# Pooled attention and sticky expert routing: another order of issue in the attention, and a new expert's first weights split ahead of the turning of the next rows

## The chip, the cores and the metric

The kernel runs on one core of one Trainium2 chip. The metric is the device time of one execution in microseconds (us); the number given for a kernel is the median of its runs. The core has five engines with an instruction stream each: PE (TensorE), DVE (VectorE), ACT (ScalarE), POOL (GpSimd) and SP (SyncE, which here only starts DMA transfers). Streams wait for one another by semaphores.

## The reference, cut to what matters

Attention runs over keys and values that are averaged in groups of 8 along the sequence; its output x (8 x 576 rows of 512) goes through a mixture of 8 experts. A token takes the expert of its own argmax, or that of the token before it, by a local gate. All is fp32.

```python
# q, k, v: 8 batches x 8 heads x 576 x 64; k_p, v_p: means over groups of 8 (72 left)
scores = scale * q @ k_p.T;  attn = softmax(scores);  x = attn @ v_p
logits = x @ w_gate;  local = sigmoid(x @ w_local)
for b in range(8):
    prev_e = -1
    for s in range(576):
        fresh_e = argmax(logits[b, s])
        e = fresh_e if s == 0 or local[b, s] < 0.5 else prev_e
        prev_e = e
        h = maximum(x[b, s] @ w1[e], 0)        # w1[e]: 512 x 1024
        out[b, s] = softmax(logits[b, s])[e] * (h @ w2[e])   # w2[e]: 1024 x 512
```

## The kernel before

**Three stages.** The attention takes the span's first 245 us or so. Blocks of 256 tokens of the most populous expert follow, in code written out (to about 315 us), and then a loop of 20 blocks over all experts.

**The attention's order of issue** is a list of words, `PLAN`, which `run(PLAN)` walks: `do(op, n)` issues one small step, and every engine executes its own instructions in the order in which the list puts them. There are 20 units, five for each pair of batches. A word is a step and a number: `lq`, `lk`, `lv` load a unit's data (SP's queue); `vp`, `vt`, `vc`, `vm`, `vl`, `vd` make pooled values and their routing logits (`vaug`); `kp` pools keys; `sc`, `mx`, `sb`, `ex` are scores, maximum, subtraction and exponential (ACT L508); `T0` to `T2` turn the probabilities on PE, `T0c` and so on copy the turned ones (`aT`, ACT L376); `v0` to `v2` multiply by the values (PE L566), `v0c` and so on copy the results (`osb`); `fs`, `fp`, `fd` sum, scale and store rows of x. A `.d` or `.p` behind the name puts a step on DVE or POOL instead of its usual engine.

Routing words stand among them, per pair of batches: `rA` (argmax and gate as small DVE operations, L621 to L636, with transposes on PE L645) to `rP` (places of tokens), then `s`, the scatters of row ids (POOL L702). `ch` and `er` choose the most populous expert; `w1`, `w2` load its weights and `p1`, `p2` split them: ACT rounds them to a high part (L212, L217), and POOL subtracts to get the low part (L213, L218). `il`, `ga` load the ids of a static block and gather its rows (POOL L270), `XR` reorders the gathered rows on ACT (L281), `X0`, `X1` turn and split them for PE. `XR:0` is the first static block, `XR:1` the second. `PLAN_B` and `PLAN_C` list the static blocks in the same way.

Every fp32 product is made from three products of high and low parts, so an expert block needs x and the weights split.

**The loop.** A block is two groups of 128 rows, or one. Its steps, in the order of the code: `l1_two` or `l1_one` (first layer, PE L330 and L332, or L957 and L963), `next_x` for the block to come (DVE turns its gathered rows, L318; ACT and DVE split them, L323 and L324; DVE sums the ids of the block after that, L304 and L305), `fetch` (eight gathers of that later block on POOL, L314), and `rest` (second layer in two halves, PE L351; scaling, DVE L1065; scattered stores on POOL, L1076). Where the next block has another expert, `rest` also splits the new weights behind the second half of the second layer, `weights1` (ACT L212 and DVE L213) and then `weights2` (ACT L217 and DVE L218), inside an `If`, and starts the loads of the expert after that. Every engine in the `If` reads the flag `chg` from a table and branches on it, whether the expert changes or not.

Of the kernel before, what the change touches and what calls it, by code (L numbers as in the profile page):

```python
# [51 lines left out]


PLAN = plan("""
wa:0 lv:0 lv:1 wa:1 lv:2 lk:0 lk:1 lq:0 lk:2 lq:1 lq:2 lc:0 lq:3 pf:0 vp:2 vt:2 vc:2 vm:2 kp:0 vp:0 lk:3 kp:1 vp:1
lv:3 vt:0 lk:4 sc:0 vc:0 vm.d:0 mx:0 lv:4 vt:1 lv:5 lq:4 vm:1 sb:0 kp:2 ex:0 sc:2 lk:5 vl:0 T0:0 vd:0 mx:2 vl:2
T0c:0 vc:1 vd:2 T1:0 sb:2 vl:1 T1c:0 T2:0 vd:1 T2c:0 ex:2 v0:0 kp:3 v1:0 v0c:0 lk:6 vp.d:3 v1c:0 v2:0 lv:6 vt:3
v2c:0 sc:1 vm:3 vc:3 fs:0 vl:3 fp:0 mx:1 lq:5 lq:6 T0:2 vp:5 T0c:2 T1:2 vd:3 sb:1 vt:5 T1c:2 v0:2 vm:5 vc:5 fd:0
vp:4 vl:5 v0c:2 T2:2 vd:5 v1:2 kp:4 ex:1 lv:7 vt:4 lv:8 lk:7 vp:6 vc:4 vm.d:4 T2c:2 vl:4 v1c:2 T0:1 vd:4 kp:5 T0c:1
T1:1 lv:9 kp:6 lk:8 T1c:1 T2:1 v2:2 T2c:1 sc:3 v2c:2 lk:9 fs:2 v0:1 lq:7 mx:3 fp:2 v0c:1 v1:1 fd.p:2 sb:3 vp:8 v1c:1  # L60
v2:1 sc:4 v2c:1 ex:3 fs:1 vt:6 lq:8 vt:8 mx:4 fp:1 vc:6 vc:8 T0:3 sb:4 vm:8 fd:1 vm:6 T0c:3 T1:3 kp:7 vp:7 T1c:3
T2:3 vl:6 T2c:3 sc:5 vd:6 ex:4 lk:10 T0:4 mx:5 vp:9 lv:10 lv:11 lq:9 T0c:4 T1:4 vl:8 T1c:4 vt:7 vd:8 sb:5 vc:7 v0:3
vm:7 lv:12 kp:8 v0c:3 v1:3 ex:5 lk:11 v2:3 v1c:3 vl:7 v2c:3 v0:4 fs:3 v0c:4 v1:4 vd:7 fp:3 T0:5 v1c:4 fs:4 fd.p:3
T0c:5 T1:5 rA:0 fp:4 T1c:5 T2:5 sc:6 fd.p:4 T2c:5 vp:11 vt:9 lq:10 mx:6 vt:11 vc:9 vl:9 vc:11 vm:11 rT0:0 vm:9 vd:9
sb:6 vl:11 vp:10 rT1:0 vd:11 ex:6 rS0:0 v0:5 rS1:0 vp:12 lv:13 lv:14 kp:9 v0c:5 v1:5 v1c:5 v2:5 lv:15 lk:12 vt:10
v2c:5 T0:6 vm:10 vc:10 fs:5 vl:10 T0c:6 T1:6 vd:10 fp:5 v0:6 T1c:6 vp:14 fd:5 kp:10 T2:6 v0c:6 v1:6 vp:13 T2c:6
lk:13 v1c:6 v2:6 rT2:0 v2c:6 lv:16 sc:7 lv:17 fs:6 rS2:0 fp:6 lq:11 mx:7 rE:0 rL:0 fd.p:6 sb:7 vt:12 vt:13 vm:12
rO:0 ex:7 sc:8 vm:13 vp:17 rR:0 vc:12 mx:8 lq:12 vc:13 T0:7 vp:15 rV:0 T0c:7 T1:7 v0:7 T1c:7 rP:0 lv:18 T2:7 v0c:7
v1:7 sb:8 s:0 T2c:7 v1c:7 v2:7 s:0 kp:11 ex:8 sc:9 s:0 mx:9 lq:13 lk:14 v2c:7 T0:8 s:0 fs:7 T0c:8 T1:8 s:0 sb:9 v0:8
T1c:8 fp:7 T2:8 s:0 v0c:8 fd:7 v1:8 T2c:8 ex:9 s:0 v2:8 v1c:8 s:0 T0:9 v2c:8 fs:8 s:0 T0c:9 T1:9 vl:12 sc:10 T1c:9  # L70
vd:12 fp:8 v0:9 fd.p:8 mx:10 lq:14 v0c:9 v1:9 sb:10 vl:13 v1c:9 vt:14 vt:15 vc:14 vm:14 fs:9 sc:11 ex:10 vd:13 fp:9
rA:1 fd.p:9 vl:14 vc:15 T0:10 vm:15 lq:15 vp:16 T0c:10 T1:10 vd:14 mx:11 v0:10 T1c:10 T2:10 sb:11 v0c:10 vp:18 v1:10
lv:19 lv:20 T2c:10 v1c:10 v2:10 ex:11 vl:15 lv:21 vt:16 vd:15 vt:17 vm.d:16 sc:12 vm:17 v2c:10 vc:16 fs:10 vc:17
vl:16 lq:16 T0:11 vd:16 fp:10 mx:12 vl:17 T0c:11 T1:11 fd.p:10 vd:17 sb:12 v0:11 vp:20 T1c:11 T2:11 kp:12 vp:19
v0c:11 v1:11 T2c:11 ex:12 kp:13 lk:15 v2:11 rT0:1 v1c:11 lv:22 lv:23 v2c:11 fs:11 rT1:1 sc:13 rS0:1 fp:11 rS1:1
fd.p:11 rT2:1 lq:17 T0:12 rS2:1 mx:13 rE:1 vp:23 T0c:12 T1:12 rL:1 T1c:12 sb:13 vp:21 T2:12 v0:12 T2c:12 rO:1 ex:13
rR:1 v1:12 rV:1 v0c:12 v1c:12 v2:12 rP:1 T0:13 v2c:12 s:0 ch:0 T0c:13 T1:13 s:0 v0:13 fs:12 T1c:13 er:0 s:0 T2:13
kp:14 v0c:13 v1:13 fp:12 T2c:13 w1:0 w2:0 w1:1 v1c:13 v2:13 s:0 fd:12 sc:14 v2c:13 s:0 fs:13 vt:18 lq:18 vt:19
vc:18 s:0 vl:18 mx:14 vt:20 p1:0 w1:2 sb:14 vc:19 vd:18 sc:15 p2:0 vm.d:20 vm.d:18 vm.d:19 ex:14 vl:19 mx:15 p1:1 w1:3
lq:19 T0:14 vd:19 T0c:14 sb:15 p1:2 vc:20 kp:15 T1:14 T1c:14 v0:14 ex:15 v1:14 v0c:14 vl:20 v1c:14 T0:15 vd:20 fs:14  # L80
s:0 p1:3 T1:15 rA:2 T0c:15 sc:16 T1c:15 T2:15 vt:21 T2c:15 mx:16 s:0 vt:23 vc:21 vl:21 vc:23 rT0:2 s:0 vd:21 sb:16
vl:23 fp:13 rT1:2 il:0 il:1 vd:23 ex:16 vm.d:23 fp:14 sc:17 fd:13 vm:21 fd:14 rS0:2 T0:16 rS1:2 ga:0 XR:0 T0c:16
T1:16 mx:17 T1c:16 T2:16 T2c:16 sb:17 v0:15 vp:22 v0c:15 v1:15 ex:17 v2:15 w2:1 w2:2 w2:3 v1c:15 vt:22 v2c:15 rT2:2
vm:22 vc:22 fs:15 vl:22 T0:17 vd:22 fp:15 rS2:2 v0:16 p2:1 fd:15 v1:16 v0c:16 p2:2 v2:16 v1c:16 T1:17 p2:3 sc:18
v2c:16 rE:2 fs:16 T0c:17 T1c:17 rL:2 mx:18 T2:17 v0:17 T2c:17 rO:2 fp:16 sb:18 v0c:17 v1:17 fd.p:16 rR:2 v1c:17
v2:17 ex:18 rV:2 X1:0 X1c:0 T0:18 v2c:17 sc:19 T0c:18 fs:17 X0:0 X0c:0 T1:18 fp:17 v0:18 T1c:18 fd.p:17 rP:2 T2:18
v0c:18 v1:18 mx:19 s:0 T2c:18 sb:19 v1c:18 v2:18 s:0 ex:19 s:0 v2c:18 T0:19 fs:18 s:0 T0c:19 T1:19 T1c:19 v0:19 s:0
v0c:19 v1:19 s:0 v1c:19 s:0 ga:1 XR:1 ma:0 fs:19 s:0 s:0 fp:18 fp:19 fd:18 fd:19
""")
# [12 lines left out]
def moe_attention(ctx: ExitStack, tc: tile.TileContext, q, q_st, k, v, w_gate, w_local, w1, w2, out):  # L102
# [1017 lines left out]
    def weights1(nx):  # L1120
        for c in range(KD):
            split1(rw1(c), c, nc.vector)
        load1(rw1, nx)
# [3 lines left out]
            split2(rw2(c), c, nc.vector)  # L1127
        load2(rl2, nx)

    def rest(j, single):  # L1130
# [15 lines left out]
        with tc.If(chg > 0):  # L1146
# [73 lines left out]
```

## Time and profile before

| what | value |
|---|---|
| median of 3 runs (lowest, highest) | 791.36 us (790.5, 796.12) |
| profiled execution: its time, its span | 789.34 us, 786.9 us |
| mean granted TensorE clock | 0.899 |
| stages of the span | attention to 245, static blocks to 315, loop to 787 us |
| blocks in the loop | 20, of which 5 with one group of rows |
| changes of expert among them | 6, before the blocks that start at 412, 479, 525, 551, 643 and 661 us |

A row of the timeline gives the start, the duration, the engine, the line in the kernel, the operation with its tiles and shapes, the count, and in brackets the idle time of the engine ahead of it with what ended it. A row of the windows view gives a stretch, its length, the busy time and count of PE, PEld (weight load), DVE, ACT and POOL, the granted clock, the share of DMA time and GB/s. "PEclk" on the page is the granted clock of each fortieth of the span in tenths. Times are from the start of the span.

### The profile page before, as it was taken

Reading aid. Unit: us, or ns where it says so; the run is one execution under the profiler, and the core shown is the slowest. Engines: PE = TensorE matmul, PEld = TensorE weight load, DVE = VectorE, ACT = ScalarE, POOL = GpSimd, SP = SyncE. Lnnn points to the kernel's source line nnn. Section 1 sums busy time; section 2 is a strip of 40 time slices with the busy share of each in tenths; the row PEclk is TensorE's granted clock in tenths of the full one; section 3 lists DMA queues with packets and bytes.
Section 4 is the critical chain, followed back from the end, with each engine's and each line's share of the span. In section 5 each row is a group of like instructions: output and inputs, shape, how many; then the busy total and the mean of one; then the engine's idle time right before and its main releaser. Section 6 shows DMA issues by size and latency. Waiting matters only on the chain. (4 is left out here: it accounts for less than half of the span.)

```text
span 786.9 us, 14972 instructions
## 1 busy us (share of the span) xinstructions
PE 657.8 (84%) x3588; PEld 545.8 (69%) x3589; DVE 450.9 (57%) x1058; ACT 273.8 (35%) x613; POOL 437.8 (56%) x659
## 2 busy tenths in 40 slices
...
PEclk9998779866798999899999899899989997999995
...
GB/s 236 284 317 248 234 174 180 146 202 54 122 54 67 31 203 106 44 41 42 42 56 242 52 36 213 83 91 197 256 54 35 42 132 223 176 50 42 42 41 29
DMA packets 49377, 96.77 MB, mean 123 GB/s; under 512 B 22974, under 2 KB 22978, under 8 KB 49348
## 3 DMA queue, kind: packets, MB, share of 16 engines
...
q8 instruction: 14, 0.23, 0.1%
...
## 5 line engine op out<-in xcount | busy, mean ns | idle before, releaser
L314 POOL DMA_INDIRECT kt<-x_rows,idk x168 | 180.1, 1072 | 49.7 <-issue 43.4
L330 PE MATMUL hp<-x,w1h 128*128 128x512 f32 x376 | 147.1, 426 | 11.7 <-ACT w1h L212 5.0
L351 PE MATMUL o_ps<-w2h,ht_h 128*128 128x512 f32 x312 | 123.9, 397 | 2.7 <-PEq L1140 1.0
L351 PE MATMUL o_ps<-w2l,ht_h 128*128 128x512 f32 x312 | 122.8, 394 | 0.0
L351 PE MATMUL o_ps<-w2h,ht_l 128*128 128x512 f32 x312 | 122.8, 394 | 0.0
L332 PE MATMUL hp<-x,w1l 128*128 128x256 f32 x376 | 112.4, 299 | 8.0 <-DVE w1l L213 3.1
L330 PEld LDWEIGHTS hp<-x,w1h 128*128 128x128 f32 x376 | 76.5, 204 | 32.5 <-issue 11.2
L338 DVE TENSOR_TENSOR hs<-hp,hs 128x256 f32<-128x256 f32 x94 | 39.2, 423 | 100.1 <-ACT hs L337 66.3
L337 ACT COPY hs<-hp 128x256 f32<-128x256 f32 x94 | 34.3, 367 | 165.3 <-PE hp L332 46.1
L332 PEld LDWEIGHTS hp<-x,w1l 128*128 128x128 f32 x376 | 76.8, 204 | 13.4 <-issue 12.7
L566 PE MATMUL op<-vaug,aT 128*128 128x148 f32 (+4 forms) x448 | 75.4, 346 | 4.1 <-ACT aT L376 4.0
L566 PEld LDWEIGHTS op<-vaug,aT 128*128 128x128 f32 (+1 forms) x448 | 69.3, 208 | 9.5 <-ACT aT L376 5.2
L351 PEld LDWEIGHTS o_ps<-w2h,ht_h 128*128 128x128 f32 x312 | 59.5, 191 | 16.9 <-issue 4.5
L342 ACT ACTIVATE ht_h<-hs 128x256 fp32r<-128x256 f32 x136 | 57.0, 419 | 35.4 <-DVE hs L338 21.3
L351 PEld LDWEIGHTS o_ps<-w2h,ht_l 128*128 128x128 f32 x312 | 59.3, 190 | 12.8 <-DVE ht_l L343 0.2
L351 PEld LDWEIGHTS o_ps<-w2l,ht_h 128*128 128x128 f32 x312 | 59.5, 191 | 11.7
L1065 DVE TENSOR_SCALAR ob<-o_ps,m_a 128x512 f32<-128x512 f32 x42 | 31.4, 749 | 59.1 <-PE hp L332 16.2
L343 DVE SCALAR_TENSOR_TENSOR ht_l<-hs,ht_h 128x256 fp32r<-128x256 f32 x136 | 57.0, 419 | 8.0 <-ACT ht_h L342 7.1
L1086 POOL TENSOR_TENSOR kt<-idk,zf 128x8 f32<-128x8 f32 x20 | 8.6, 432 | 90.4 <-DVE idk L305 86.5
L1076 POOL DMA_INDIRECT out<-ob,m_e x42 | 44.8, 1067 | 25.0 <-issue 25.0
L702 POOL DMA_INDIRECT ids<-pm,pos x36 | 35.5, 988 | 19.1 <-DVE pos L699 9.4
L323 ACT CAST x<-qt 128x512 fp32r<-128x512 f32 x40 | 22.8, 618 | 60.3 <-DVE qt L318 60.3
...
## 6 DMA issues: line engine op xcount, KB each, us to landing
...
```

What stands on the lines that cost most here:

```text
L314: nc.gpsimd.indirect_dma_start(out=xk[:, j, :], out_offset=None, in_=x_pc[0:4 * rows], in_offset=bass.IndirectOffsetOnAxis(ap=idk[:, j:j + ...
L330: nc.tensor.matmul(out=ps, lhsT=W1[0][:, kk, f * P:(f + 1) * P], rhs=xt[:, kk].rearrange("p i n -> p (i n)"), start=(kk == 0), stop=False, ...
L332: nc.tensor.matmul(out=ps[:, 0:2 * P], lhsT=W1[1][:, kk, f * P:(f + 1) * P], rhs=xt[:, kk, 0, :], start=False, stop=(kk == KD - 1), skip_g ...
L337: nc.scalar.copy(out=hb[:, 0, :], in_=ps[:, 2 * P:])
L338: nc.vector.tensor_tensor(out=hb[:, 1, :], in0=ps[:, 0:2 * P], in1=hb[:, 0, :], op=ALU.add)
L342: nc.scalar.activation(out=ht[0][:, f, :], in_=hb, func=AF.Relu)
L343: nc.vector.scalar_tensor_tensor(out=ht[1][:, f, :], in0=hb, scalar=0.0, in1=ht[0][:, f, :].bitcast(F32), op0=ALU.max, op1=ALU.subtract)
L351: nc.tensor.matmul(out=to[h], lhsT=ht[i][:, kk, h * P:(h + 1) * P], rhs=W2[j][:, kk, :], start=(n == 0), stop=(n == 3 * KF - 1))
L566: nc.tensor.matmul(out=out, lhsT=lhs, rhs=rhs if len(out.shape) == 3 else rhs.rearrange("p s x -> p (s x)"), start=all(x[0] != n for x in ...
L702: nc.gpsimd.indirect_dma_start(out=ids[u % 4].rearrange("t m w -> (t m) w"), out_offset=bass.IndirectOffsetOnAxis(ap=pos[:, u:u + 1], axis=0),
L1065: nc.vector.tensor_scalar(out=ob[:, h, :], in0=o_ps[h], scalar1=m_a[:, h, 1:2], scalar2=None, op0=ALU.mult)
L1076: nc.gpsimd.indirect_dma_start(out=outv, out_offset=bass.IndirectOffsetOnAxis(ap=m_e[h][:, 0:1], axis=0), in_=ob[:, h, :], in_offset=None, ...
```

## The change

**The list.** `PLAN` is written in another order, with the same steps, and `XR:1` moves from its end to `PLAN_B`, behind `rO:3`. Some steps go to another engine: on balance one `vp` and three `vm` more stand on DVE, and one `fd` more on POOL. The new text is one line longer, so every later line number is one higher, and nine higher at the end. One line of it, where the first static block's rows are gathered and reordered:

```diff
@@ PLAN (all of its lines differ; one is shown)
+v1:14 T1c:15 T2:15 w1:3 vl:21 v1c:14 sc:17 vd:21 T2c:15 ex:16 fs:14 vl:23 ga:0 fp:14 vd:23 p1:2 v0:15 rA:2 T0:16
+v0c:15 p1:3 v1:15 T0c:16 T1:16 v1c:15 mx:17 XR:0 v2:15 rT0:2 fd:14 v2c:15 sb:17 T1c:16 rT1:2 vp:22 rS0:2 fs:15
...
@@ PLAN_B
-L1:4 rR:3 ct:0 rV:3 rP:3 h0:4 h1:4 s:0 s:0 s:0 s:0 s:0 s:0 s:0 s:0 s:0 L1:5 tc:0 cn:0 i1:0 h0:5 h1:5
+XR:1 L1:4 rR:3 ct:0 rV:3 rP:3 h0:4 h1:4 s:0 s:0 s:0 s:0 s:0 s:0 s:0 s:0 s:0 L1:5 tc:0 cn:0 i1:0 h0:5 h1:5
```

**The loop.** The flag is read right behind the first layer, and `weights1` is done there, ahead of `next_x`; `weights2` stays where it was.

```diff
-    def rest(j, single):
-        chg = entry(j + 1, 2, (EN.Activation, EN.DVE, EN.Pool, EN.SP), 1)
-        nx = entry(j + 1, 3, (EN.SP,), E - 1)
+    def changes(j):
+        return entry(j + 1, 2, (EN.Activation, EN.DVE, EN.SP), 1), entry(j + 1, 3, (EN.SP,), E - 1)
+
+    def first(chg, nx):
+        with tc.If(chg > 0):
+            weights1(nx)
+
+    def rest(j, single, chg, nx):
         meta_shift()
...
         with tc.If(chg > 0):
-            weights1(nx)
             weights2(nx)
...
     l1_two()
+    chg, nx = changes(1)
+    first(chg, nx)
     next_x()
     fetch(1)
-    rest(1, None)
+    rest(1, None, chg, nx)
...
+            chg, nx = changes(iv)
+            first(chg, nx)
             next_x()
             fetch(iv)
-            rest(iv, two)
+            rest(iv, two, chg, nx)
```

**ACT's instructions around `XR:0`.** `at` are probabilities, `aT` the turned ones, `osb` results of the attention, `brow` a row of the routing. Before:

```order
L508 ACTIVATE at<-ap 128x2x2x216
L508 ACTIVATE at<-ap 128x2x80
L508 ACTIVATE at<-ap 128x128
L648 COPY brow<-tp 2x256
L281 COPY qt<-qt 128x4x4x32 x2
L376 COPY aT<-tp 128x512 x2
L376 COPY aT<-tp 128x128
L376 COPY osb<-op 128x444
```

ACT in the changed kernel, at the same copies of the gathered rows (now L282):

```order
L213 CAST w1h<-kt 128x1024
L377 COPY osb<-op 128x444
L213 CAST w1h<-kt 128x1024
L377 COPY aT<-tp 128x512
L377 COPY osb<-op 128x444
L282 COPY qt<-qt 128x4x4x32 x2
L377 COPY osb<-op 128x2x148
L377 COPY aT<-tp 128x512
```

Five copies of ACT, of which two are splits of weights, now stand between the point of the gather and the copies of the gathered rows; before, none did.

**POOL's instructions around the splits of the first expert's weights.** `ids` are the scattered row ids, `w1l` and `w2l` the low parts, `xs` scaled rows of x, `vaug` the pooled values; the last row is the gather of the first static block. Before:

```order
L702 DMA ids_65<-pm,pos 65536x2
L213 TENSOR_TENSOR w1l<-kt,w1h 128x1024
L218 TENSOR_TENSOR w2l<-vt_in,w2h 128x1024
L213 TENSOR_TENSOR w1l<-kt,w1h 128x1024 x2
L702 DMA ids_66<-pm,pos 65536x2
L213 TENSOR_TENSOR w1l<-kt,w1h 128x1024
L702 DMA ids_67<-pm,pos 65536x2
L702 DMA ids_64<-pm,pos 65536x2
L603 TENSOR_TENSOR xs<-osb,rr 128x512
```

POOL in the changed kernel, from the last scatter of the second pair on:

```order
L703 DMA ids_64<-pm,pos 65536x2
L214 TENSOR_TENSOR w1l<-kt,w1h 128x1024
L445 TENSOR_TENSOR vaug_210<-vs,mk 128x2x64
L604 TENSOR_TENSOR xs<-osb,rr 128x512
L214 TENSOR_TENSOR w1l<-kt,w1h 128x1024
L219 TENSOR_TENSOR w2l<-vt_in,w2h 128x1024
L267 MEMSET qt 128x1024
L271 DMA qt<-x_rows,idr_191 128x512 x2
L604 TENSOR_TENSOR xs<-osb,rr 128x256
L214 TENSOR_TENSOR w1l<-kt,w1h 128x1024 x2
```

Four splits stood in a row among the scatters; now all scatters of that pair come first, three splits come ahead of the gather and two right behind it, beside the routing of the third pair.

**DVE's instructions in the loop**, from the end of a first layer on. Before, the turning of the next rows (L318) is the first thing after the branch of the first layer, and the splits (L213) come behind the scaling (L1065):

```order
L1177 UNCONDITIONAL_BRANCH
L318 REGISTER_ALU
L318 STREAM_TRANSPOSE qt<-kt 128x8x4x32
...
L1065 TENSOR_SCALAR ob<-o_ps_2481,m_a 128x512
L1146 COMPARE_AND_BRANCH
L213 REGISTER_ALU
L213 TENSOR_TENSOR w1l<-raw_3004,w1h 128x1024
```

DVE in the changed kernel:

```order
L1184 UNCONDITIONAL_BRANCH
L224 ISA
L224 TENSOR_LOAD tab
L1135 COMPARE_AND_BRANCH
L214 REGISTER_ALU
L214 TENSOR_TENSOR w1l<-raw_3001,w1h 128x1024
...
L1135 UNCONDITIONAL_BRANCH
L319 REGISTER_ALU
L319 STREAM_TRANSPOSE qt<-kt 128x8x4x32
```

A read of the flag and a branch now stand ahead of the turning in every block, and four subtractions more where the expert changes; the branch behind the scaling is still there, for `weights2` alone.

More of the change, by code (lines that the diff above doesn't have):

```diff
@@ L85 @@
[L85 to L88, printed above, removed]
+wa:0 lv:0 lv:1 lv:2 lk:0 wa:1 lk:1 lk:2 lq:0 lc:0 lq:1 lq:2 pf:0 lq:3 vp:0 vp.d:2 lv:3 vt:0 vc:0 vm:0 vt:2 kp:0
@@ new lines @@
+vc:2 vm:2 vp:1 lk:3 kp:1 lv:4 vt:1 lv:5 kp:2 vm:1 lk:4 sc:0 lk:5 vl:0 mx:0 lq:4 vc:1 vd:0 sb:0 vl:2 vd:2 ex:0 vl:1
+sc:2 vd:1 T0:0 mx:2 T0c:0 T1:0 vp:3 sb:2 v0:0 T1c:0 T2:0 kp:3 v1:0 v0c:0 T2c:0 lv:6 vt:3 v1c:0 v2:0 vm.d:3 vp:5
+vc:3 lk:6 vl:3 v2c:0 sc:1 vp:4 ex:2 vd:3 fs:0 vt:5 lq:5 lq:6 T0:2 mx:1 vc:5 fp:0 lv:7 lv:8 vt:4 vl:5 vm.d:5 vc:4
+vm:4 T0c:2 vd:5 kp:4 vl:4 fd.p:0 T1:2 vd:4 vp:6 v0:2 kp:5 lk:7 T1c:2 T2:2 v0c:2 v1:2 T2c:2 kp:6 lv:9 lk:8 v1c:2
+v2:2 sb:1 lk:9 vt:6 v2c:2 vm:6 fs:2 ex:1 sc:3 fp:2 vc:6 mx:3 lq:7 T0:1 vp:8 T1:1 T0c:1 sb:3 fd.p:2 v0:1 T1c:1 vp:7
@@ new lines @@
+T2:1 kp:7 v1:1 v0c:1 T2c:1 ex:3 v2:1 vp:9 lv:10 lv:11 lk:10 v1c:1 sc:4 v2c:1 T0:3 lq:8 fs:1 vl:6 lv:12 T0c:3 T1:3
+vd:6 vt:8 fp:1 mx:4 T1c:3 vm.d:8 vc:8 sb:4 T2:3 fd.p:1 vt:7 T2c:3 kp:8 vl:8 vc:7 sc:5 vm:7 ex:4 vd:8 kp:9 lk:11
+v0:3 lq:10 T0:4 v0c:3 mx:5 vp:11 lk:12 v1:3 T0c:4 vp:10 T1:4 sb:5 v1c:3 v2:3 T1c:4 vl:7 v2c:3 vt:9 vd:7 ex:5 vt:11
+fs:3 sc:6 lv:14 lv:13 vm:11 vc:11 vm.d:9 vc:9 fp:3 vl:11 lq:9 mx:6 T0:5 vt:10 fd.p:3 T0c:5 vd:11 v0:4 kp:10 vc:10
+vm:10 T1:5 v0c:4 sb:6 vp:12 lk:14 v1:4 T1c:5 kp:11 vl:9 v1c:4 T2:5 sc:7 T2c:5 ex:6 lv:15 fs:4 vt:12 lq:11 lk:13
@@ new lines @@
+T0:6 vd:9 fp:4 rA:0 vl:10 T0c:6 fd.p:4 vm:12 vc:12 T1:6 vp:14 T1c:6 T2:6 vp:13 T2c:6 lv:16 vd:10 v0:5 mx:7 rT0:0
+v0c:5 sb:7 lv:17 v1:5 rS0:0 vp:15 rT1:0 v1c:5 ex:7 v2:5 rS1:0 rT2:0 v2c:5 sc:8 lv:18 rS2:0 fs:5 rE:0 rL:0 lq:12
+mx:8 fp:5 T0:7 v0:6 rO:0 fd.p:5 T0c:7 sb:8 rR:0 v0c:6 vp:17 v1:6 rV:0 T1:7 v1c:6 rP:0 v2:6 T1c:7 T2:7 sc:9 v2c:6
+s:0 T2c:7 ex:8 fs:6 vl:12 vt:14 s:0 v0:7 mx:9 vc:14 fp:6 vd:12 T0:8 sb:9 v0c:7 s:0 v1:7 fd:6 T0c:8 vm.d:14 kp:12
+s:0 T1:8 v1c:7 v2:7 s:0 kp:13 T1c:8 lk:15 T2:8 vl:14 s:0 T2c:8 vt:13 v2c:7 sc:10 ex:9 fs:7 s:0 vc:13 v0:8 lq:13
```

47 lines of the change are left out of this document (17 added, 30 removed).

## The prediction

> **What bounds the kernel now.** I read the page, then the busy time by stretches, then the waits and the timeline at the places that the change touches.
>
> ```profile
> span 786.9 us, 14972 instructions
> PE 657.8 (84%) x3588; PEld 545.8 (69%) x3589; DVE 450.9 (57%) x1058; ACT 273.8 (35%) x613; POOL 437.8 (56%) x659
> PEclk9998779866798999899999899899989997999995
> ...
> 140.00:160.00 20.00, 18.07 (x147) 15.94 (x146) 15.19 (x46) 8.04 (x20) 12.68 (x16) 0.83 0.46 151
> 160.00:180.00 20.00, 13.30 (x77) 10.41 (x78) 19.71 (x28) 9.51 (x20) 13.87 (x9) 0.59 0.49 174
> 180.00:200.00 20.00, 11.41 (x78) 8.43 (x76) 14.89 (x30) 3.27 (x10) 9.86 (x11) 0.67 0.35 106
> 200.00:220.00 20.00, 16.52 (x109) 15.47 (x110) 7.12 (x13) 11.28 (x24) 12.90 (x11) 0.76 0.20 67
> 315.00:787.00 472.00, 403.25 (x1848) 328.58 (x1848) 242.84 (x511) 156.63 (x330) 261.75 (x412) 0.92 0.28 94
> ```
>
> PE is the bound: busy for 84% of the span, and for 403.25 of the 472 us of the loop, at a granted clock of 0.92. The hole is in the attention, from 160 to 220 us: PE is busy for 13.30 + 11.41 + 16.52 = 41.2 of 60 us, and the clock falls to 0.59. In the first of these stretches DVE is busy for 19.71 of 20 us. So the order of issue is worth looking at there, and the loop only where PE waits for an x or for a weight.
>
> **Reordering behind the gather (`XR:0`).** The first row is the gather of the first static block, the second ACT's reordering of it, then PE, DVE and two ACT copies.
>
> ```profile
> 197.14 1.09 POOL L270 DMA_INDIRECT qt<-x_rows,idr  x1 [9.32 <-DVE idr L264]
> 201.06 0.62 ACT L281 COPY qt<-qt 128x512 f32<-128x512 f32 x1 [5.79 <-DMA qt<-x_rows,idr]
> 203.15 0.48 PE L524 MATMUL tp<-ident,at 128*128 128x128 f32 x1 [5.93 <-ACT aT L376]
> 209.50 0.17 DVE L583 TENSOR_SCALAR rr<-osb 128x16 f32<-128x16 f32 x1 [10.53 <-ACT osb L376]
> 205.97 0.53 ACT L376 COPY osb<-op 128x444 f32<-128x444 f32 x1 [2.05 <-PE op L566]
> 209.61 1.04 ACT L217 CAST w2h<-vt_in 128x1024 fp32r<-128x1024 f32 x1
> 179.42 1.08 ACT L376 COPY aT<-tp 128x512 f32<-128x512 f32 x2
> ```
>
> ACT's stream stands for 5.79 us at the gathered rows. The copies of `aT` are queued behind, so PE stands 5.93 us, and DVE 10.53 us. From the gather's start (197.14) to its use (201.06) pass 3.9 us. In the changed order two weight casts, two `osb` and one `aT` stand between: 2 x 1.04 + 2 x 0.53 + 0.54 = 3.7 us of ACT work, about what the transfer takes. The gap goes but for ACT's own second copy: **-5.0 us** (0 to -5.9: nothing, if these five copies themselves wait for PE; all of it at best).
>
> **Reordering of the second static block (`XR:1`).**
>
> ```profile
> 243.31 0.62 ACT L281 COPY qt<-qt 128x512 f32<-128x512 f32 x1 [0.71 <-DMA qt<-x_rows,idr]
> 244.23 0.42 DVE L338 TENSOR_TENSOR hs<-hp,hs 128x256 f32<-128x256 f32 x1 [1.92 <-ACT qt L281]
> 244.71 0.79 PE L330 MATMUL hp<-x,w1h 128*128 128x512 f32 x1 [1.65 <-DVE hs L338]
> ```
>
> The first static block's `hs` stood behind these copies. With `XR:1` behind `rO:3` the wait of PE, 1.65 us, goes, and nothing later than it is due before the second block's x: **-1.65** (0 to -1.65).
>
> **Splits beside DVE.** The first two rows are the same DVE operation beside POOL's splits and without them; the third is the first of the four splits.
>
> ```profile
> 163.22 10.90 DVE L444 TENSOR_TENSOR vaug<-vs,mk 128x128 f32<-128x128 f32 x5
> 18.07 1.37 DVE L444 TENSOR_TENSOR vaug<-vs,mk 128x128 f32<-128x128 f32 x2
> 163.95 2.36 POOL L213 TENSOR_TENSOR w1l<-kt,w1h 128x1024 fp32r<-128x1024 f32 x1
> 175.69 0.70 PE L428 MATMUL rt<-wg,vT 64*128 64x72 f32 x2 [2.53 <-DVE vaug L436]
> 183.81 2.67 DVE L635 SCALAR_TENSOR_TENSOR ab<-bm,ac,nbm 128x2 f32<-128x2 f32 x1
> 241.95 0.22 DVE L635 SCALAR_TENSOR_TENSOR ab<-bm,ac,nbm 128x2 f32<-128x2 f32 x1
> 188.60 0.67 PE L428 MATMUL rt<-wg,vT 64*128 64x72 f32 x2 [4.58 <-DVE vaug L436]
> ```
>
> Five `vaug` took 10.90 us, where two took 1.37, so 3.4 for five: 7.5 us of DVE are lost beside four splits, 1.9 a split. PE paid 2.53 us of it behind the next `vaug`; that gap I count as gone, since these five now stand beside scatters: **-2.5** (0 to -7.5). The second gap, 4.58, hangs on the routing of the second pair, whose tiny L635 took 2.67 us beside POOL's scaling against 0.22 alone. Such a meeting recurs with the third pair, so I take nothing for it (+4.6 if doubled, -4.6 if gone).
>
> The Trainium skill (SBUF — State Buffer, Who interferes with whom) says that a DVE instruction with two SBUF inputs and a GpSimd instruction that reads SBUF exclude one another, and that the later one waits for the whole of the other. The 2.67 us agree in kind, and this rule speaks against the change: it is the first rival below.
>
> **The clock** at that place. The three stretches ran at 0.59, 0.67 and 0.76, the one before at 0.83. At 0.83 their 41.2 us of PE work would take about 41.2 x 0.67 / 0.83 = 33.3, some 8 us less (0.67: mean of the three). As only two of the gaps close, I take a quarter: **-2.0** (0 to -8).
>
> The Trainium skill (TensorE: Matmul & The Clock Gate, Part 1: The HAM clock gate) has PE at half rate after about 3.4 us of idling, until it has been busy for as long. By it the vanished 5.93 us gap alone would return about 1.7 us, half of such a window (an estimate from that page).
>
> **The start.** `vp:2` goes to DVE, ahead of `kp:0`, and `sc:0` now stands behind the turning of `vp:1`.
>
> ```profile
> 18.10 1.32 PE L461 MATMUL sp<-kdz,qt 128*128 128x144 f32 x4
> 35.48 1.91 DVE L389 TENSOR_REDUCE vs<-vt_in 128x128 f32<-128x1024 f32 x1
> 14.16 1.35 DVE L402 TENSOR_REDUCE kd<-kk 128x144 f32<-128x1152 f32 x1 [7.67 <-DMA kk<-in_k]
> ```
>
> The half-wide sum on DVE costs half of 1.91, so the keys' sums behind it, and the scores of 18.10, come **+1.0** us later (0 to +2, if the wait for the keys hides it, or if `vp:1` is later still).
>
> **The loop**: a clean change of expert, then a block whose x was late, then PE's waits in the loop (total, times, longest).
>
> ```profile
> 402.99 0.43 DVE L343 SCALAR_TENSOR_TENSOR ht_l<-hs,ht_h 128x256 fp32r<-128x256 f32 x1 [0.24 <-ACT ht_h L342]
> 404.23 1.25 DVE L318 STREAM_TRANSPOSE qt<-kt 128x1024 f32<-128x1024 f32 x1 [0.81 <-DVE ht_l L343]
> 407.43 3.90 ACT L212 CAST w1h<-raw 128x1024 fp32r<-128x1024 f32 x4 [0.70 <-ACT x L323]
> 409.44 4.64 DVE L213 TENSOR_TENSOR w1l<-raw,w1h 128x1024 fp32r<-128x1024 f32 x4
> 412.25 0.39 PE L330 MATMUL hp<-x,w1h 128*128 128x512 f32 x1
> ...
> 488.44 0.95 POOL L314 DMA_INDIRECT kt<-x_rows,idk  x1 [0.31 <-issue]
> 494.42 1.25 DVE L318 STREAM_TRANSPOSE qt<-kt 128x1024 f32<-128x1024 f32 x1 [5.21 <-DMA out<-ob,m_e]
> 497.34 0.47 PE L330 MATMUL hp<-x,w1h 128*128 128x512 f32 x1 [3.32 <-DVE x L324]
> 500.05 0.55 PE L332 MATMUL hp<-x,w1l 128*128 128x256 f32 x1 [2.23 <-DVEq L1146]
> 661.10 0.76 PE L330 MATMUL hp<-x,w1h 128*128 128x512 f32 x1 [5.03 <-ACT w1h L212]
> ...
> PE hp L332 <- DVE w1l L213: 3.1, 7, 1.3
> PE hp L332 <- issue: 2.5, 5, 0.7
> ```
>
> What goes: PE's waits for low parts of weights, 3.1 + 2.5 us (those put to "issue" lie in the same first products), and the 2.23 at 500.05, where PE waited until DVE had passed a branch that it didn't take. That is -7.8.
>
> What comes: at a change `w1h` starts where the first layer ends, 402.96 + 0.70 = 403.7, the subtractions one cast later, at 404.7, and end 4.64 later at 409.4; with the present 0.81 us ahead of it the turning starts at 410.2, **6.0 later**. From the turning at 494.42 to PE's start at 497.34 passed 2.9 us, so x is there at 413.1, where PE comes at 412.25: 0.85 late, at five changes +4.2. The gathers on POOL hang on the same ids and come as much later, less about 0.6 for those that no longer run beside a DVE split: 5.4. In front of a two-group block with a whole second layer of 11 us that is hidden; behind a one-group block it isn't. The block of 497.34 already hung on such a gather (488.44 + 0.95, and 5 us of landing, gives 494.42): +5.4. That of 661.10 did too, but its x was there at 660, and it waited for weights that are now early: 5.4 - 2.0 for this = +3.4. Sum of the loop: -7.8 + 4.2 + 5.4 + 3.4 = **+5.2**; ends: -7.8, if x is in time everywhere, and +13.0, if the waits for weights only change their name.
>
> The flag's read and branch also come ahead of the turning in the other 14 blocks, at most the 0.81 us that stand ahead of the turning at 404.23, where a branch lies too; x was at PE well ahead of the end of a second layer there (404.23 + 2.9 = 407.1, against 412.25), so nothing; without that cover it would be 14 x 0.81 = 11.3.
>
> **Sum.** -5.0 - 1.65 - 2.5 - 2.0 + 1.0 + 5.2 = -4.95 us on the profiled execution's 789.34: 784.4. The median is 791.36, 2.0 above it; on the median the forecast is **786.4 us**, own range 778 to 795.
>
> **Rivals.**
> 1. *Slower: the splits meet the routing.* Five of POOL's splits now run beside the third pair's routing, a chain of DVE operations with two inputs each, on which `sc` and the scatters wait. Price: 5 x 1.9 = 9.4, a second 4.58-like stall by 5.1 (2.67 and its neighbours against some 0.2 each), and the clock's 2.0 that doesn't return: 786.4 + 16.5 = 803. It beats the savings from 4.95 us of delay on; for: the 10.90 row; against: the routing has pauses while PE transposes, in which a split can run. By the rule of the Trainium skill above (SBUF — State Buffer, Who interferes with whom) a split delays such a chain by its whole length, 2.36, and the time would be 805.
> 2. *No change: the next wait takes over.* DVE had 19.71 of 20 us to do; if PE, let off `aT`, waits for `at` and `osb` as long, -5.0, -2.5 and -2.0 fall away: 786.4 + 9.5 = 796.
> 3. *Much faster: x is in time in the loop.* Without the 13.0 us of later x, 773; with 160 to 220 us packed like the stretch ahead of it (41.2 / 18.07 x 20 = 45.6, so -14.4 for -9.5), 768.5. For: the 0.85 is inside my error; against: the gather's chain.
> 4. *The new list amounts to the same* because other queues set the pace: 791.
>
> **How the numbers follow.** My forecast 0.42, the first rival 0.19, the second 0.14, the third 0.23, the last 0.02. A measurement here can tell about 1%, 7.9 us, from no change: below 783.4 lie the third rival and under half of my own case, 0.41; above 799.3 most of the first rival, 0.18; between, 0.41. The range that leaves out 2 in 10 takes in most of the third and half of the first: 770 to 802.
>
> **What would show it.** Right: ACT's wait at L282 below 2 us and no PE gap of 5.93 there; no 1.65 gap ahead of the first static block; the weights' low parts off PE's waits, with x (L325) in their place at 412 and the next changes; the turning 6 us later at a change, and PE standing longest at the blocks behind the one-group blocks near 497 and 661. Wrong: an attention that ends later than 245 us with DVE's `ab` steps at 2 us each (rival 1), the same sum of PE gaps from 160 to 220 under other names (2), or no wait for x at a change (3). I would be most wrong if a gap opens in the attention where before has none, since I priced only the places that were late before.

## The result, and the profile after

| kernel | median | lowest to highest | runs |
|---|---|---|---|
| before | 791.05 us | 790.5 to 796.12 | 4 |
| changed | 801.85 us | 798.82 to 804.76 | 4 |

The ratio is 1.0131, with a 95% interval of 1.0091 to 1.017: the change costs 1.3% where 0.6% less was forecast. Here and below a ratio is taken over the fast runs alone, those within 1.5% of the fastest of the same kernel, while a median is over all runs. The profiled execution of the changed kernel took 803.99 us, its span 802.3. Its page, then the three stretches of the hole in the attention:

```profile
span 802.3 us, 14899 instructions
PE 654.8 (82%) x3588; PEld 543.6 (68%) x3589; DVE 456.2 (57%) x1062; ACT 272.2 (34%) x613; POOL 426.2 (53%) x652
```

```profile
160.00:180.00 20.00, 15.67 (x136) 13.81 (x136) 16.48 (x31) 10.32 (x23) 13.37 (x11) 0.77 0.61 197
180.00:200.00 20.00, 15.35 (x93) 13.45 (x92) 13.92 (x26) 8.16 (x19) 11.07 (x10) 0.67 0.48 154
200.00:220.00 20.00, 17.41 (x148) 15.33 (x148) 15.07 (x38) 12.96 (x27) 13.83 (x10) 0.96 0.11 43
```

PE's work is the same (654.8 us busy, before 657.8), and the hole is closed by some two fifths: PE is busy for 48.4 of the 60 us, before for 41.2 (11.6 us without work for 18.8), at clocks of 0.77, 0.67 and 0.96 for 0.59, 0.67 and 0.76. So the time was lost elsewhere. Read from the timelines, with "list" for all up to the last product of the static blocks:

| piece | before | changed | difference | forecast |
|---|---|---|---|---|
| start to the last static second layer | 314.9 | 302.3 | -12.6 | -10.15 |
| from there to the loop's first product | 4.92 | 8.80 | +3.9 | 0 |
| the loop, from its first product to the end | 467.1 | 491.2 | +24.1 | +5.2 |

The list did slightly more than forecast; the loop, and the step into it, lost it all.

**Where the loop lost it.** PE's waits, first of the changed kernel, then of before (in each row the total, the times and the longest):

```profile
PE tp L964 <- ACT hs L961: 18.7, 5, 6.8
PE hp L331 <- issue: 9.5, 16, 1.2
PE hp L333 <- issue: 9.3, 17, 1.7
PE hp L958 <- DVEq L1181: 8.8, 1, 8.8
PE hp L331 <- DVE x L325: 5.5, 4, 2.4
PE o_ps L352 <- PEq L1146: 4.6, 2, 4.1
PE hp L958 <- ACT x L324: 4.1, 2, 2.1
```

```profile
PE hp L963 <- ACT hs L960: 8.0, 2, 4.1
PE hp L330 <- ACT w1h L212: 5.0, 1, 5.0
PE tp L332 <- issue: 3.4, 6, 0.9
```

The 8.8 is the step into the loop. The other rows of the whole view, put together by releaser: waits for x are 9.6 us now (5.5 + 4.1) and were 3.3; waits for weights were 10.8 (2.2 of it for a branch of DVE) and are gone; waits put to "issue", to "remote", to PE's own sequencer or to `hs` of the one-group first layers are 48.5 us now and were 26.3 (without 4.9 us at the step into the loop). +6.3 - 10.8 + 22.2 and 2.6 of small rows give +20.3 of the loop's +24.1; PE's busy time in it, 405.66 us where before had 403.25, makes most of the rest. The forecast had priced the first two of these groups, and the third decided.

Block by block, from the end of one second layer to the end of the next, +17.9 of the +24.1 stands where the first weights' splits were moved: at the six blocks ahead of which the expert changes, and at the one behind the first of them that has one group (497 in before). The two of one group take 10.1 and 9.5 us more (before 15.1 and 13.3), and the blocks behind these give back 7.1 and 5.4. Of these 10.1 and 9.5, 2.1 each are a wait for x, 2.7 and 2.4 a longer first layer, 2.4 and 3.6 a wait ahead of the second layer, and the rest a longer second layer. The waits ahead of the second layer, two rows of the changed kernel and then the place of the second in before:

```profile
492.79 0.77 PE L352 MATMUL o_ps<-w2h,ht_h 128*128 128x512 f32 x1 [2.94 <-remote]
666.54 0.77 PE L352 MATMUL o_ps<-w2h,ht_h 128*128 128x512 f32 x1 [4.10 <-PEq L1146]
650.35 0.47 PE L351 MATMUL o_ps<-w2h,ht_h 128*128 128x512 f32 x1 [0.50 <-issue]
```

**What the third group is.** A one-group first layer of the loop in the changed kernel (of a block without a change of expert, so that no split runs beside it; it took 13.96 us, in before 11.48): PE's product, ACT's activation of what PE made, PE's turning of that, and POOL meanwhile.

```profile
586.34 0.39 PE L958 MATMUL hp<-w1h,x 128*128 128x512 f32 x1
593.26 0.60 ACT L961 ACTIVATE hs<-hp 128x512 f32<-128x512 f32 x1 [8.46 <-remote]
594.00 1.09 PE L964 MATMUL tp<-ident,hs 128*128 128x128 f32 x4 [6.83 <-ACT hs L961]
589.05 0.94 POOL L315 DMA_INDIRECT kt<-x_rows,idk  x1 [0.30 <-issue]
591.30 1.04 POOL L1077 DMA_INDIRECT out<-ob,m_e  x1 [0.68 <-issue]
```

PE's last product started at 586.34 and ended at 586.7 (the start is recorded, the end modelled), and ACT had nothing else to do, yet ACT took it up 6.5 us later. In that time POOL ran its row of gathers (580.14 to 589.99) and a store (591.30). The semaphore events of the trace show why: PE had signalled the end of its products one by one, some 0.23 us apart, until 581.08, a microsecond into POOL's row of gathers; from 583.80 on the recorded ones are 583.80, 584.49, 585.93, 587.35, 588.07, 588.80, 590.22, 590.25, 591.64, 591.68, 591.71, and at the end 593.10, 593.13, 593.17, 593.20, 593.24. Signals 0.034 us apart, of products that follow one another 0.23 us apart, read as old ones let go together: **the work was done, and the news of it stood in line.** The step into the loop is the same thing:

```profile
301.89 0.39 PE L352 MATMUL o_ps<-w2h,ht_l 128*128 128x512 f32 x1
310.19 0.75 DVE L1066 TENSOR_SCALAR ob<-o_ps,m_a 128x512 f32<-128x512 f32 x1 [11.42 <-remote]
311.07 0.77 PE L958 MATMUL hp<-w1h,x 128*128 128x512 f32 x1 [8.80 <-DVEq L1181]
```

PE's second layer ended at 302.3, DVE learned of it at 310.1. PE also stands in the middle of a first layer with nothing to wait for:

```profile
417.01 0.40 PE L331 MATMUL hp<-x,w1h 128*128 128x512 f32 x1 [1.18 <-issue]
```

I read the "issue" gaps as PE stopped by its own signals not yet sent. That is a reading: the trace names no releaser there.

The Trainium skill (SBUF — State Buffer, Who interferes with whom) says that PE and ACT never wait on anyone. That is about ports of SBUF, and the products of the block shown bear it out, which start 0.23 us apart beside the gathers; what waits here is the signal behind them, which no sentence of that section covers.

### The profile page after: what moved, and what is told of

It is laid out like the page before. It is cut to its first block, busy times and chain, and to the rows that moved or that the text cites. A ratio compares the mean times of both kernels' runs of the same rounds, so it can differ in the third digit from the quotient of the medians.

```text
span 802.3 us, 14899 instructions
## 1 busy us (share of the span) xinstructions
PE 654.8 (82%) x3588; PEld 543.6 (68%) x3589; DVE 456.2 (57%) x1062; ACT 272.2 (34%) x613; POOL 426.2 (53%) x652
## 5 line engine op out<-in xcount | busy, mean ns | idle before, releaser
L315 POOL DMA_INDIRECT kt<-x_rows,idk x168 | 166.7, 992 | 49.9 <-issue 43.2
L331 PE MATMUL hp<-x,w1h 128*128 128x512 f32 x376 | 143.6, 417 | 17.5 <-issue 9.5
L352 PE MATMUL o_ps<-w2h,ht_h 128*128 128x512 f32 x312 | 127.8, 409 | 10.2 <-PEq L1146 4.6
L352 PE MATMUL o_ps<-w2l,ht_h 128*128 128x512 f32 x312 | 125.9, 404 | 0.0
L352 PE MATMUL o_ps<-w2h,ht_l 128*128 128x512 f32 x312 | 125.6, 402 | 0.0
L333 PE MATMUL hp<-x,w1l 128*128 128x256 f32 x376 | 109.4, 291 | 9.3 <-issue 9.3
L331 PEld LDWEIGHTS hp<-x,w1h 128*128 128x128 f32 x376 | 74.1, 197 | 41.9 <-issue 21.8
L333 PEld LDWEIGHTS hp<-x,w1l 128*128 128x128 f32 x376 | 74.5, 198 | 12.8 <-issue 12.4
L344 DVE SCALAR_TENSOR_TENSOR ht_l<-hs,ht_h 128x256 fp32r<-128x256 f32 x136 | 59.5, 437 | 7.5 <-ACT ht_h L343 6.8
L383 POOL TENSOR_TENSOR t<-vt_in 128x512 f32<-128x512 f32 (+1 forms) x22 | 24.7, 1122 | 42.7 <-DMA vt_in<-in_v 42.2
```

Source lines behind the costliest of these rows:

```text
L315: nc.gpsimd.indirect_dma_start(out=xk[:, j, :], out_offset=None, in_=x_pc[0:4 * rows], in_offset=bass.IndirectOffsetOnAxis(ap=idk[:, j:j + ...
L331: nc.tensor.matmul(out=ps, lhsT=W1[0][:, kk, f * P:(f + 1) * P], rhs=xt[:, kk].rearrange("p i n -> p (i n)"), start=(kk == 0), stop=False, ...
L333: nc.tensor.matmul(out=ps[:, 0:2 * P], lhsT=W1[1][:, kk, f * P:(f + 1) * P], rhs=xt[:, kk, 0, :], start=False, stop=(kk == KD - 1), skip_g ...
L344: nc.vector.scalar_tensor_tensor(out=ht[1][:, f, :], in0=hb, scalar=0.0, in1=ht[0][:, f, :].bitcast(F32), op0=ALU.max, op1=ALU.subtract)
L352: nc.tensor.matmul(out=to[h], lhsT=ht[i][:, kk, h * P:(h + 1) * P], rhs=W2[j][:, kk, :], start=(n == 0), stop=(n == 3 * KF - 1))
L383: nc.gpsimd.tensor_tensor(out=t4[:n, 0:m], in0=src[:, :, 0:256], in1=src[:, :, 256:512], op=ALU.add)
```

## The experiments

A sitting is a group of kernels that ran on one chip one after another, with runs of the kernel before among them. They turned out to be of two kinds. In the one, before takes 787 to 793 us, and pairs of PE's signals in the loop under 0.05 us apart number 442 in its trace and 534 in the changed kernel's. In the other it takes 741 to 744 us, and no trace has such a pair. I call them sittings with late signals and with signals in time, and a ratio is read only within its sitting.

One caution goes with all that follows. Traces of the first kind also hold fewer records of signals: 7,957 updates by all engines and DMAs of the changed kernel in the first result, 11,814 of the same kernel in time (e8). So single times of signals are only those that were kept. The argument rests on what is recorded in both: when the engine that waits starts, and the time of the whole run.

| kernel | signals | median us | before us | ratio, 95% interval |
|---|---|---|---|---|
| change, first result | late | 801.85 | 791.05 | 1.0131 (1.0091 to 1.017) |
| change (e5) | late | 789.81 | 788.04 | 1.0077 (1.003 to 1.0123) |
| change (e8) | in time | 728.9 | 743.88 | 0.9784 (0.9726 to 0.9843) |
| list alone (e1, e6, e11) | in time | 733.35, 733.26, 732.1 | 744.13, 743.88, 744.41 | 0.9857, 0.9857, 0.9836 (0.978 to 0.991 in all) |
| loop alone (e2, e7, e10, e14) | in time | 739.65, 740.59, 737.44, 740.9 | 744.13, 743.88, 744.41, 740.65 | 0.9916, 0.9948, 0.9938, 0.9979 (0.987 to 1.002 in all) |
| loop alone (e16) | late | 816.09 | 793.48 | 1.0227 (1.0087 to 1.0368) |
| no gathers in the loop (e3, e9, e12; one run each) | in time | 702.99, 703.66, 703.35 | 744.13, 743.88, 744.41 | none |
| no gathers in the loop (e17) | late | 712.02 | 786.79 | 0.9071 (0.8977 to 0.9165) |
| pauses between gathers (e4) | in time | 811.41 | 744.13 | 1.091 (1.0841 to 1.0979) |
| first weights behind the gathers (e13, e15) | in time | 724.2, 723.72 | 744.41, 740.65 | 0.9723, 0.9775 (0.966 to 0.981 in both) |
| first weights behind the gathers (e18) | late | 777.76 | 786.87 | 0.9873 (0.983 to 0.9916) |

### One part alone, and the change without its gathers

The list alone is the new `PLAN` and `PLAN_B` with the loop of before. The loop alone is the old list with the new loop. The third kernel is the change without the loop's gathers:

```diff
-        def fetch(b):
+        def fetch(b, rows=True):
...
-            gather(js=range(0, 1))
+            if rows:
+                gather(js=range(0, 1))
...
-            gather(js=range(1, TB))
+            if rows:
+                gather(js=range(1, TB))
...
-            fetch(iv)
+            fetch(iv, False)
```

> The new list with the old loop. In the trace of the change the loop's first product comes 8.8 us earlier than before (311.1 against 319.8) and the loop takes 491 us against 467. If the list gave the first and the loop edit took the second, this kernel takes 791 - 8.8 = 782 us, with a loop of 467 to 470. If the new list itself lengthens the loop (other tiles, other places in the code), it takes 795 to 802.

> The old list with the new loop. If the loop edit costs the 24 us, 791 + 20 to 24 = 811 to 815 us. If the list does, 788 to 796. My own sum of the loop said +5, so 796.

> The change without the gathers of rows inside the loop (later blocks work on the rows that were there; left out: the fetching of the rows). Theory S: PE's products are done in time, but their signals come late while POOL issues gathers, and PE stops when too many are outstanding; then without gathers every first layer of two groups takes 11.6 us instead of 13 to 16, ACT's wait for the one-group blocks' second half (18.7 us of PE in five) goes to nearly zero, and the loop falls from 491 to about 430. Theory X: the loop lost its time to an x that comes late behind the splits; then at the six changes PE still waits for x by the same 0.4 to 2.4 us, and the first layers keep most of their length, since the waits of PE inside them have nothing to do with the gathers: loop 470 or more.

This sitting had signals in time, which none of the expectations had reckoned with: both parts alone were faster than before (0.9857 and 0.9916), and before itself took 744.13 us. So it couldn't say where the loss came from. It showed what the parts are worth without late signals, and gave a first time without the gathers, 702.99 us. (In the later sitting with both, the gathers' part is 25.2 us: 728.9 less 703.66.)

### Pauses between the gathers

If DVE's splits beside the gathers are what spaces them and lets signals pass, small work of POOL between gathers should do the same. Two additions of 128x120 were put ahead of each of the last six gathers of a row of eight:

```diff
+            if len(js) < TB and j > 1:
+                for _ in range(2):
+                    nc.gpsimd.tensor_tensor(out=idle[1], in0=idle[0], in1=idle[0], op=ALU.add)
```

> The change with two small POOL additions (about 0.6 us) ahead of each of the last six gathers of a block. Theory S: signals get through between the gathers, so PE isn't stopped in the first layers: 802 falls to 770 to 785, though the gathers end 4 us later. Theory X: gathers that end later make x later still at the blocks behind one-group blocks: 803 to 812.

A miss: this sitting had signals in time, so there was nothing to let pass, and the pauses only cost: 9.1% more than before, and 82 us more than the change takes in time (728.9, e8). The waits of PE and of DVE in the loop:

```profile
PE hp L334 <- DVE x L328: 54.3, 11, 10.2
```

```profile
DVE qt L322 <- DMA kt<-x_rows,idk: 101.6, 17, 11.4
```

With a gather every 2.05 us POOL's row of gathers became the bound, DVE waited 101.6 us for rows and PE 54.3 for x. Whether pauses help where signals are late was not tried again.

### The change once more, beside before alone

> The change as it is, once more. On the chip of the four runs above the kernel before takes 744 us and no signal of PE comes late; the new list alone took 0.986 of that and the new loop alone 0.992. If both add up, the change takes 0.986 x 0.992 = 0.978 there, 728 us, the opposite of the first result. Where PE's signals come late behind gathers (kernel before 791 us), it takes 1.013 again, 802 us.

Another chip, late signals: 1.0077. This ratio hangs on one short run of before, 775.35 us; the medians, 789.81 and 788.04, differ by 0.2%. So a loss is not shown a second time, but neither is the gain of 2% that the change has in time. The loop took 479.5 us here and the step into it 7.0 (before had 467.1 and 4.9 in its one trace, of the first sitting), and at the seven blocks named above it took 12.8 us more than before did, elsewhere as long.

### The parts and the change in one sitting

> The new list with the old loop, a second time, beside the change and the new loop alone. Theory S (PE's signals come late while POOL gathers, on some chips): on a chip where the kernel before takes 788 to 791 us, this one takes 10 to 13 us less, ratio 0.984 to 0.988; on a chip where it takes 744, 0.986 as in the first run. If the list gains only where signals are in time, the ratio is 1.00 on the former.

> The old list with the new loop, a second time. Theory S: where signals come late, +18 to +24 us, ratio 1.023 to 1.030, since the splits that spaced out the gathers no longer stand beside them; where they come in time, 0.992 as in the first run. Theory X (late x alone) gives the same ratio on either chip, about 0.99.

> The change beside its two parts. Late signals: 1.008 to 1.013, and the sum of the two parts' differences within 4 us. Signals in time: 0.978, as list and loop add up.

> The change without the gathers of rows inside the loop (later blocks work on the rows that were there), a second time. Theory S on a chip with late signals: no first layer of two groups over 12.3 us, no wait of PE for ACT in the one-group blocks, total 700 to 710 as on the chip of the first run (703), though the change itself takes 60 us more there. If it is some other slowness of that chip, 740 or more remains without any gather.

Signals in time, and now the same change is **2.2% faster** than before. In this sitting its two parts add: 0.9857 x 0.9948 = 0.9806, against 0.9784. The step into the loop, in the change:

```profile
302.12 0.39 PE L352 MATMUL o_ps<-w2h,ht_l 128*128 128x512 f32 x1
302.61 0.75 DVE L1066 TENSOR_SCALAR ob<-o_ps,m_a 128x512 f32<-128x512 f32 x1 [3.63 <-PE o_ps L352]
303.22 0.47 PE L958 MATMUL hp<-w1h,x 128*128 128x512 f32 x1 [0.71 <-DVEq L1181]
```

The same code, the same gathers alongside, and PE's gap is 0.71 us instead of 8.80. Next, the loop: PE's waits of the list alone (old loop), then of the change, then the two rows that hold most of the last.

```profile
PE hp L333 <- DVEq L1147: 6.5, 4, 2.1
PE hp L331 <- ACT w1h L213: 4.8, 1, 4.8
PE hp L331 <- ACTq L1147: 4.0, 2, 3.1
PE hp L333 <- DVE w1l L214: 2.7, 5, 1.2
```

```profile
PE hp L331 <- DVE x L325: 19.4, 6, 9.8
```

```profile
462.99 0.77 PE L331 MATMUL hp<-x,w1h 128*128 128x512 f32 x1 [5.03 <-DVE x L325]
615.66 0.76 PE L331 MATMUL hp<-x,w1h 128*128 128x512 f32 x1 [9.80 <-DVE x L325]
```

The waits for weights and for the branch that goes untaken, 18.0 us, are gone, as forecast (I had 7.8 of them, from a trace with late signals). x is late for 19.4 us in their place, and 14.8 of that stand at the two blocks behind one-group blocks that the prediction named, where the list alone already waits 3.1 us (for ACT's branch) and 4.8 (for a weight). All waits of the view together rise by 3.1 us, and PE's busy time falls from 386.05 to 377.33, so the loop is about 5 us shorter (430.1 to 425.1).

> The old list with the new loop, on whatever chip comes. Where PE's signals come late behind gathers (kernel before 788 to 791 us), theory S: ratio 1.02 to 1.03, as the change there is 1.008 to 1.013 with a list that gains 0.986. Rival: the list loses there and the loop is neutral, 0.99 to 1.00. Where signals come in time (744): 0.992 to 0.995 once more.

> The new list with the old loop. Late signals, theory S: 0.982 to 0.990. Rival: 1.00 to 1.015, the list itself loses. In time: 0.986 once more.

> The change without the gathers of rows inside the loop (later blocks work on the rows that were there). Late signals, theory S: 700 to 712 us, so that the gathers and nothing else make such a chip slow. Rival: the chip is slower in itself: 740 or more. In time: 703 once more.

Again signals in time, again both parts faster than before (0.9938, 0.9836), and no gathers 703.35.

### The first weights behind the gathers

The waits for weights can be saved without the lateness of x: the flag is read and the first weights are split behind the turning and the gathers, yet ahead of the scaling. All else is the change, and the same is done ahead of the loop.

```diff
-            chg, nx = changes(iv)
-            first(chg, nx)
             next_x()
             fetch(iv)
+            chg, nx = changes(iv)
+            first(chg, nx)
```

> The new list, with the flag read and the first weights split behind the next rows' turning, splitting and gathers, but still ahead of the second layer's scaling. In time: x is no longer late (19.4 us of PE in the change), and the waits for the branch and for weights' low parts (about 9 us with the old loop) mostly go: 0.968 to 0.976, faster than change and list. Late signals, theory S: the splits stand beside the gathers again, so the list's gain stays: 0.975 to 0.99. Theory X gives the same on either chip.

The best kernel so far: 0.9723. PE's waits in its loop:

```profile
PE hp L331 <- ACT w1h L213: 3.6, 1, 3.6
PE hp L331 <- DVE x L325: 2.7, 2, 2.0
PE hp L333 <- DVEq L1135: 0.8, 2, 0.4
```

Both kinds of wait are small at once: x 2.7 us instead of 19.4, and the rows that had taken 18.0 us are down to 5.3 (3.6 + 0.8, and 0.9 in w1l's own row).

> The old list with the new loop, on whatever chip comes. Late signals, theory S: 1.02 to 1.03. Rival (the list loses there): 0.99 to 1.00. In time: 0.992 to 0.995.

> The new list with the first weights split behind the gathers. Late signals, theory S: 0.975 to 0.99. If the place of the splits doesn't matter there: 1.005 to 1.015, as the change. In time: 0.972 once more.

The loop alone was within the error here (0.9979), the version behind the gathers again 2.3% faster.

### The disputed parts under late signals

Late signals had come up only where a single kernel was run beside before, so each of the next three was run so.

> The old list with the new loop. Late signals (kernel before 788 to 791 us), theory S: 1.02 to 1.03, the loop edit is what makes the change slower there. Rival: 0.99 to 1.00, then the list is. In time: 0.992 to 0.998.

> The change without the gathers of rows inside the loop (later blocks work on the rows that were there). If the kernel before takes 788 to 794 us here (late signals), theory S: 700 to 712 us, 90 us less than the change there, and first layers of 11.5 us; rival (the chip is slower in itself): 740 or more. If 744: 703 once more, which tells nothing.

> The new list with the first weights split behind the gathers. If the kernel before takes 788 to 794 us here (late signals), theory S: 0.975 to 0.99, 7 to 20 us less, since the splits stand beside the gathers again; if their place doesn't matter there: 1.005 to 1.015, as the change. If 744: 0.972 to 0.978 once more.

Late signals in all three. **Loop alone: 1.0227**, the same kernel on the same chip that had given 0.9979. The interval's lower end is 1.0087, so the loss is the loop's. Its waits, in a trace of 819.31 us, the upper end of its four runs (805.95 to 820.76):

```profile
PE tp L963 <- ACT hs L960: 13.2, 4, 6.6
PE hp L332 <- issue: 9.2, 17, 1.0
PE hp L330 <- issue: 8.1, 14, 1.2
```

These are the names that had grown in the change, and 19.8 of the 25.4 us that its loop is longer than before's stand at the same seven blocks. **No gathers in the loop: 0.9071**, 712 us, with these waits left:

```profile
PE hp L958 <- issue: 7.0, 1, 7.0
PE hp L331 <- DVE x L325: 5.0, 3, 3.4
PE tp L964 <- ACT hs L961: 2.4, 5, 0.5
```

Without gathers no two of PE's signals in the loop are under 0.05 us apart, the "issue" rows inside first layers are gone, and the longest wait for `hs` is 0.5 us instead of 6.8. The one 7.0 left is the step into the loop, beside the gathers ahead of it, which this kernel keeps. As a control, the same omission in time saves 25 us of the loop (425.1 to 400.3); here it saves 77 to 89 (479.5 and 491.2 to 402.6). Each of these loops is one trace, and the chips differ. So some 52 to 64 us of a run under late signals hang on the gathers beyond what they cost otherwise: **that it is the gathers behind which PE and its readers stand is shown.** Not all of these us are waits: the same 1848 products of the loop keep PE busy for 405.66 us at a granted clock of 0.91 in the first result, for 377.33 at 0.96 in time, and for 377.60 at 0.98 here. By what path a gather holds a signal back, no run tells.

**First weights behind the gathers: 0.9873**, where the change gave 1.0077 and 1.0131. Its loop takes 467.6 us, as long as the 467.1 of before; first layers of one group 9.82 us, where before had 9.73 and the change 11.40 and 10.82. One gather of it at a change of expert:

```profile
403.42 1.94 POOL L315 DMA_INDIRECT kt<-x_rows,idk  x1 [0.30 <-issue]
```

**Why the place of the splits matters.** In this kernel four of the eight gathers at that change take 1.55 to 1.97 us instead of 0.95, where DVE's subtractions run beside them (399.8 to 404.5 and 406.4 to 411.1; the gather between, at 405.67, takes 0.95). Before had three of 1.96 to 1.97. The changed kernel has one: its first weights' splits are over when its gathers start, and the second weights' run beside only a few.

The one-group first layers, without the first block of the loop, show what goes with this. In before and in the version behind the gathers, the gathers start 2.2 to 4.4 us ahead of each of them. The two at a change of expert, where three or four gathers are lengthened, take 9.07 and 7.28 us in before, 7.15 and 7.43 in the other (with signals in time 7.1 to 7.4). The two without a change, where none is, take 11.68 and 11.48, 13.12 and 12.59. In the two late traces of the changed kernel, with one lengthened gather or none and a start of the gathers near that of the layer, all four take 9.72 to 13.96. The pairs of signals under 0.05 us apart go the same way: 442 and 388 in these two kernels, 514 to 550 in the three late traces with the splits ahead. The two-group layers don't part as clearly: at the change shown the changed kernel took 15.4 us in one late trace and 12.9 in the other, before 12.05.

I take it that a split which holds a gather up also lets signals pass. The version behind the gathers gave back the loss, as this has it, but it also brought x back in time, and the run made to tell these apart (pauses) fell into a sitting in time. So this last step is supported and not shown. That DVE and POOL hold each other up is what the Trainium skill (SBUF — State Buffer, Who interferes with whom) says of a DVE instruction with two inputs beside a GpSimd instruction that reads SBUF, and the 1.96 for 0.95 agree, if a gather's reading of its ids counts as that; that it may do good has no place there.

**Open:** why signals are late in some sittings. It isn't the chip, since chip 14 had both kinds. All five late ones had one kernel beside before and all four in-time ones two to four; chance would part nine so in 1 of 126 ways, and nothing here says what else would. With a third of the signals' records missing there, I can't rule out that the recording has a part in it: every run on record comes with a span and a clock, so none is surely free of recording. The list alone under late signals was not measured; its part ends 12.6 and 13.1 us earlier in the two late traces of the change.

## Why the prediction was wrong

The wide range, 770 to 802, just held the time of 801.85, the own range of 778 to 795 didn't, and the sign was wrong. None of the rivals was the way in which it went: the first one's 803 us fits by luck, since the attention in which it puts the loss became faster.

**Right: reordering behind the gather.** ACT's copies of the gathered rows follow without idle time, and PE has no gap of 5.93 there. The five copies put between did wait meanwhile, for a load and for PE (2.15 and 3.06 us), but PE did not stand behind them.

```profile
186.56 1.16 ACT L282 COPY qt<-qt 128x512 f32<-128x512 f32 x2
```

**The second static block's reordering: the wait went, the time didn't.** It now stands beside a product of the first static block that waits for nothing, where 1.65 us had been lost. But from the first product of the static blocks to the last pass 81.1 us, before 81.3, for the second block's x now comes 0.93 us late (at 256.37). Of the 1.65 little is left, and the list's whole gain lies ahead of the static blocks: their first product starts at 221.24, before at 233.64.

```profile
235.21 1.12 ACT L282 COPY qt<-qt 128x512 f32<-128x512 f32 x2
235.22 0.80 PE L331 MATMUL hp<-x,w1h 128*128 128x512 f32 x1
```

**Wrong in size, both ways: splits and clock.** The splits' term, -2.5, did not come. They met DVE at two places: ahead of the second pair's scores (177.07), behind `vaug` of 3.15 us for two and `xs` of 1.50 beside two of the splits, and, as assumed, in the third pair's routing. PE paid 4.33 and 3.46 us, where before's two gaps were 2.53 and 4.58. The 0.7 us more is all that came of the first rival. The clock gave more than its -2.0: from 140 us to the first static product as many products (523 and 524) kept PE busy for 65.25 us at 0.85, before for 70.81 at 0.74. So the list's sum came out near by errors that offset each other.

```profile
177.07 1.33 PE L462 MATMUL sp<-kdz,qt 128*128 128x144 f32 x4 [4.33 <-DVE ap L494]
181.97 2.67 DVE L623 TENSOR_TENSOR sh<-lg,ml 128x72 f32<-128x72 f32 x1
192.62 1.33 PE L462 MATMUL sp<-kdz,qt 128*128 128x144 f32 x4 [3.46 <-DVE ap L494]
```

The start came 1.1 us later (forecast 1.0: the scores of 18.10 stand at 19.22), but that is luck: the keys' sums ended only 0.2 us later (18.24 for 18.05), and the scores waited 1.57 us for their queries' load, which the prediction left out. The sum of the list, -10.15, measured -12.6 in the first trace and -10.6 to -12.3 as the list alone in time (732.1 to 733.35 against 743.88 to 744.41).

**Wrong: the loop, +5.2 forecast, +24.1 measured.** The steps inside it were mostly there. The turning at the first change came at 402.01, 6.3 us behind the end of the first layer, before 0.8, so 5.5 later (forecast 6.0); x was late at five changes by 7.2 us in sum (forecast 4.2); the waits for weights went. The two blocks behind one-group blocks were not the ones that stood longest: PE waited 0 and 2.4 us ahead of them, before 3.3 and 5.0, and the loss lay in the one-group blocks themselves. Only in time did they stand as named, 5.03 and 9.80 us, which is 1.9 and 5.0 more than with the list alone (forecast 5.4 and 3.4). What failed is the step that priced the loop by waits that bear a name, x and weights. It put the 2.5 us of "issue" at the first products down to the weights, and left the `hs` row of 8.0 us, which was the largest in the loop and which no step of the change seemed to touch, out of the sum. I take both for late signals (for `hs` the signals of the changed kernel show it, for "issue" it is a reading), and both grew: the `hs` rows from 9.4 to 18.7 us, all "issue" in the loop from 15.9 to 22.3. One term even had its sign turned: "less about 0.6 for those that no longer run beside a DVE split" counted as a gain that the gathers run unhindered, where, if the reading above holds, the hindered gathers were the ones that let PE go on. The step into the loop was not priced at all, though before already showed its 4.9 us under "issue".

The third rival (x in time in the loop) had its premise wrong and its size not: in time the change gives 0.978, which on 791.05 would be 774, yet with x late by 19.4 us.
